# Softmax sums by products with ones, and both heads per instruction, in the first twelve attention units

## The chip, the cores and the metric

One core of a Trainium2 chip runs the whole kernel in one launch. The metric is the device time of the launch in microseconds; lower is better. Engines are TensorE (PE, with its weight loads PEld), VectorE (DVE), ScalarE (ACT), GpSimd (POOL) and SyncE (SP), which here issues the loads and stores.

## The reference

Attention over 8 batches, 8 heads, 576 positions and 64 dimensions, followed by an FFN on the 4608 x 512 result:

```python
scores = scale * np.matmul(q, k.transpose(0, 1, 3, 2))          # scale = 1/8
rel = pos[:, None] - pos[None, :]
mask_plain = (rel >= 0) & (rel < 32)                            # heads 0-3
mask_dil = (rel >= 0) & (rel < 128) & (rel % 4 == 0)            # heads 4-7
scores = np.where(masks, scores, -1e9)
attn = np.exp(scores - scores.max(-1, keepdims=True))
attn = attn / (attn.sum(-1, keepdims=True) + 1e-9)
x = (attn @ v)                                                  # to [4608, 512]
h = np.maximum(np.maximum(x @ w1, x @ w2), x @ w3)              # 512 -> 768
out = h @ w_out                                                 # 768 -> 512
```

q, k, v and the output are float32, the FFN's weights float64.

## The kernel before

**Tiling.** The positions of a batch are cut into two halves of 288 rows, and the heads into four pairs: 16 halves x 4 pairs make 64 attention units, numbered in that order. Pairs 0 and 1 are plain, pairs 2 and 3 dilated. A plain unit has three blocks of 96 queries by 128 keys for each of its two heads, a dilated one four blocks of 72 by 104 (its positions are sorted by remainder mod 4, so that the window is dense). The FFN goes over ten tiles of rows (two of 256, eight of 512), in three products of split numbers: x and the weights are kept as a float32r high part and a rest (xH and xL, wupH and wupL, wdn, h), and high x high, low x high, high x low are summed in PSUM (L815 for the up side, L870 for the down side). x lies in a ring of 1536 rows (xH, xL).

**Two kinds of units.** Units 0 to 11 (LEAN = 12) go through `dense` (L477), units 12 to 63 in pairs through `attention` and `behind` (L648, L681). `dense` puts the mask into PSUM as a product with the identity (L502), adds the scores (L507), and takes the row maxima, one instruction for each head (`most`, L525). Then it does one of two things. Units with u % 4 in (0, 2) (BLOCKWISE) scale the maxima (`eighth`, L531) and take one exponential for each block from PSUM into the buffer W, with the row sums as an accumulator output (`expo_b`, L550). The others subtract the maxima on DVE (`less`, through the helper at L361), take one exponential for each head in SBUF (`expo`, L539), and sum on DVE (`total`, L542). Both then add 1e-9 to the sums (`eps`, L570), take the reciprocals of 6 or 8 columns (`recip`, L573), multiply W by them (`norm`, POOL or DVE, L361), transpose each block on PE (L588), copy the result to PT (`turned`, L354 on ACT or L358 on DVE), and multiply with v (L602). `rounded_of` (L612) writes the output to xH and the rest to xL. Line 354 is the ACT copy helper, L358 the DVE one, L361 the two-tensor helper, whichever engine runs it.

**Weights.** `weight` (L384) is run for 18 up and 6 down weights. They come as float64 (L437), and each is put together on chip: ACT rebiases the high word (L419, into a PSUM bank cp), POOL or DVE extracts three bits of the low word (L424), DVE joins them (L428), one engine writes the high part (L354), and POOL or DVE the rest (L361). All of this lies in the first 85 us.

**What sets the order.** `Plan` (L98) holds every step with a cost for each engine that can do it (`act`, `dve`, `dve2`, `pool1`, `pool`, L364 to L378), its dependences, its buffers and a due time worked backwards from the FFN's products (`deadlines`, with UNIT_PACE, UNIT_SLACK, UNIT_LEAD for attention and WEIGHT_... for weights). `order` (L159) places the steps one by one on the engine's modelled clock, the earliest first and at equal times the one due first, and moves a step to an engine that isn't its usual one if that wins over SPILL = 3.16 us. The kernel issues in that order, and each engine's queue runs in order. PSUM has 6 banks under the tag "b" (scores, transposes, outputs, weights' cp) and 2 for the FFN. Until the first FFN product is placed, idle products (`filler`, L948) are put into PE's gaps, and 16 in a row where the modelled time passes 21 and 35 us (BURSTS).

Of the kernel before, what the change touches and what calls it, by code (L numbers as in the profile page):

```python
# [11 lines left out]
U8 = mybir.dt.uint8  # L12
# [21 lines left out]
LEAN = 12  # L34

BLOCKWISE = (0, 2)


STAGE, STAGE_H = ["wd", "h"], 4
# [26 lines left out]
class Buf:  # L66


    def __init__(self, pool, tag, limit, shape, dtype, name):
        self.pool, self.tag, self.limit = pool, tag, limit  # L70
        self.shape, self.dtype, self.name = shape, dtype, name
        self.users = 0
        self.number = None
        self.end = 0.0
        self.slot = None
        self.t = None

    def take(self):
        if self.t is None and isinstance(self.pool, list):
# [18 lines left out]
class Plan:  # L98
# [48 lines left out]
    def room(self, st, slots):  # L147
# [6 lines left out]
        for tag in set(new):  # L154
            k = new.count(tag)
            at = max(at, sorted(slots[tag])[k - 1][0] if len(slots[tag]) >= k else 1e9)
        return at

    def order(self, fill=None):  # L159
        self.deadlines()  # L160
        self.given = {}
        free = {"pe": 0.6, "act": 4.0, "dve": 4.3, "pool": 3.6, "sp": 0.6}
# [10 lines left out]
        while len(order) - fills < len(self.steps):  # L173
# [43 lines left out]
            for b in st.bufs:  # L217
                if b.slot is None:
                    free_slot = min(slots[b.tag])
                    b.slot = free_slot[1]  # L220
                    slots[b.tag].remove(free_slot)
# [22 lines left out]
            for b in st.bufs:  # L244
                b.users -= 1
                b.end = max(b.end, end)
                if not b.users:
                    slots[b.tag].append((b.end + 0.2, b.slot))
# [21 lines left out]
def tile_dilated_window_attention__then__maxout_ffn(  # L270
# [33 lines left out]
    small_c = const.tile([128, 2], F32, name="small_c")  # L304
    zero, eps_c = small_c[:, :1], small_c[:, 1:]
    nc.gpsimd.memset(eps_c, 1e-9)
    make_identity(nc, ident)
# [7 lines left out]
        "tmp": (4, [128, 512], F32),  # L315
# [10 lines left out]
    BANKS = {"b": 6, "ffn": 2}  # L326

    def buf(tag, name, shape=None, dtype=None):
        if tag in BANKS:
            return Buf(ps, tag, BANKS[tag], [128, 512], F32, name)  # L330
        if tag in KEPT:
            return Buf(KEPT[tag], tag, len(KEPT[tag]), None, None, name)
# [16 lines left out]
    for t in KEPT["W"]:  # L349
        nc.gpsimd.memset(t[:, 768:], 0.0)  # L350
# [33 lines left out]
    def weight(j, before):  # L384

        up = j < NWU
        n = 512
        f = j // 3 if up else j - NWU
        st = buf(STAGE[j % len(STAGE)] if j < STAGE_H else "wd", f"st{j}", [128, 2 * n], F32)
        res = [] if up else [wdn[f]]  # L390

        def part(z):
            return (wupL if z else wupH)[:, j] if up else wdn[f].t[:, z]

        cb, cp = buf("tmp", f"c{j}"), buf("b", f"cp{j}")

        def high():
            return st.t.rearrange("p (n t) -> p n t", t=2)[:, :, 1]

        def cf():  # L400
            return cb.t[:, :n]

        def cw():
            return cb.t.bitcast(U32)[:, :n]

        def pf():
            return cp.t[:, :n]

        def pw():
            return cp.t.bitcast(U32)[:, :n]

        def like(ap):
            return ap.rearrange("p (c m) -> p c m", c=4) if up else ap

        def rebias(_):

            nc.scalar.activation(pf(), high(), AF.Prelu, scale=REBIAS, alpha=SIGN_SHIFT)  # L419

        def low3(e):

            b = st.t.bitcast(U8).rearrange("p (n t) -> p n t", t=8)[:, :, 3]
            (nc.gpsimd if e == "pool" else nc.vector).tensor_scalar(cw(), b, 1 / 32, -31 / 64, ALU.mult, ALU.add)  # L424

        def joined(_):

            nc.vector.scalar_tensor_tensor(  # L428
                cw(), pw(), 3, cw(), op0=ALU.logical_shift_left, op1=ALU.bitwise_or
            )  # L430

        def split(e):
            copy(e, part(0), like(cf()))

        s = plan.add(
# [573 lines left out]
```

## Time and profile before

| | |
|---|---|
| time, median of 3 (lowest to highest) | 725.41 us (725.38 to 725.49) |
| the profiled execution's own time | 725.29 us |
| its span, first to last instruction | 723.4 us |
| PE, PEld busy | 710.1, 585.8 us |
| DVE, ACT, POOL busy | 364.7, 298.1, 231.7 us |
| granted PE clock | 1.00 throughout |
| moved by DMA | 57.46 MB |

Busy time is the union of an engine's instructions. PE's instructions overlap, and their ends are modelled, so the distance from one group's start to the next says more of its cost than a single duration. A row "who <- whom" in a list of waits gives total microseconds, number of times and the longest. A row of a group gives busy microseconds and mean nanoseconds, then idle time of the engine before it and what ended that.

### The profile page before, as it was taken

The page shows a single profiled execution, that of the slowest core. Times are in us where ns is not written, and L with a number is a line of the kernel's source. Part 1 is how long each engine was busy: PE and PEld are TensorE (multiplying, and loading weights), DVE is VectorE, ACT ScalarE, POOL GpSimd, SP SyncE. Part 2 cuts the span into 40 slices and gives each one's busy share as a digit, 9 for nine tenths or more (in the row PEclk, how much of TensorE's full clock was granted, in tenths as well). Part 3 has the DMA queues.
Part 4 walks back from the last instruction along what each step waited for, and adds up shares of the span by engine and source line. Part 5 has one row for each costly group of instructions (what it writes and reads, how often), then busy time and mean ns, then how long its engine had stood idle before and what let it go on. Part 6 is the DMA issues. An engine that isn't in the chain of part 4 may idle for free.

```text
span 723.4 us, 13138 instructions
## 1 busy us (share of the span) xinstructions
PE 710.1 (98%) x4750; PEld 585.8 (81%) x4750; DVE 364.7 (50%) x1419; ACT 298.1 (41%) x1104; POOL 231.7 (32%) x324
## 2 busy tenths in 40 slices
PE   8998999999999999999999999999999999999997
PEld 4677899888888888888888888888888888888886
DVE  5898665565545653666455546655565501101110
ACT  5887854444444334434444444443444311111111
POOL 4998923233223332333223232322223301200110
PEclk9999999999999999999999999999999999999999
DMA  9986232322141203121321223222300010000001
GB/s 321 342 270 201 61 91 59 93 57 65 48 131 45 77 14 108 59 62 61 101 79 58 64 87 94 58 64 72 109 23 24 13 46 1 0 30 30 0 1 58
DMA packets 30368, 57.46 MB, mean 79 GB/s; under 512 B 2912, under 2 KB 11104, under 8 KB 30304
## 3 DMA queue, kind: packets, MB, share of 16 engines
q1 hardware_dynamic: 30304, 56.63, 24.6%
q8 instruction: 37, 0.61, 0.4%
q14 instruction: 27, 0.22, 0.1%
HBM read 47.19 MB, written 9.44 MB: 78 GB/s over the span
## 4 chain that ended last, share of the span: by engine, by line
PE 89%; POOL 4%; DVE 3%; issue 2%; ACT 1%; DMA 1%; SPq 0%; POOLq 0%; DVEq 0%; ACTq 0%
PE u L815 58%; PE d L870 20%; PE s L668 5%; PE pv L774 4%; POOL c L424 1%; POOL wupL L361 1%; DMA k<-in_qk_d_dram 1%; POOL W L361 1%; DVE mx L525 1%; POOL wdn L361 1%; ACT W L550 0%; PE idle L948 0%; DVE c L428 0%; POOL h L361 0%; DVE sm L570 0%
## 5 line engine op out<-in xcount | busy, mean ns | idle before, releaser
L815 PE MATMUL u<-xH,wupH 128*128 128x512 f32 (+1 forms) x720 | 179.6, 371 | 0.4 <-DVE tmp L361 0.2
L815 PE MATMUL u<-xL,wupH 128*128 128x512 f32 (+1 forms) x720 | 178.7, 370 | 0.0
L815 PE MATMUL u<-xH,wupL 128*128 128x512 f32 (+1 forms) x720 | 177.9, 369 | 0.0
L361 DVE TENSOR_TENSOR tmp<-u,tmp 128x512 f32<-128x512 f32 (+1 forms) x120 | 76.4, 637 | 194.4 <-PE u L815 172.1
L870 PE MATMUL d<-wdn,h 128*128 128x512 f32 x648 | 151.9, 392 | 0.1
L691 ACT ACTIVATE W<-W,mx 96x128 f32<-96x128 f32 (+3 forms) x364 | 134.4, 371 | 30.9 <-DVE mx L700 30.6
L815 PEld LDWEIGHTS u<-xH,wupH 128*128 128x128 f32 x720 | 127.0, 188 | 24.5 <-ACT tmp L354 0.4
L815 PEld LDWEIGHTS u<-xL,wupH 128*128 128x128 f32 x720 | 127.4, 188 | 23.7
L815 PEld LDWEIGHTS u<-xH,wupL 128*128 128x128 f32 x720 | 127.7, 188 | 23.0
L870 PEld LDWEIGHTS d<-wdn,h 128*128 128x128 f32 x648 | 120.7, 188 | 26.4 <-POOL wdn L361 0.5
L361 POOL TENSOR_TENSOR h<-tmp,h 128x512 fp32r<-128x512 f32 (+1 forms) x60 | 71.4, 1190 | 215.4 <-ACT h L354 215.4
L762 DVE STREAM_TRANSPOSE PT<-W 32x192 f32<-32x192 f32 (+1 forms) x312 | 125.1, 401 | 16.2 <-POOL W L361 12.2
L354 ACT CAST h<-tmp 128x512 fp32r<-128x512 f32 (+1 forms) x60 | 34.6, 577 | 205.3 <-DVE tmp L361 205.3
L361 POOL TENSOR_TENSOR W<-W,sm 96x384 f32<-96x384 f32 (+3 forms) x126 | 100.3, 815 | 56.9 <-DVE sm L741 50.7
L700 DVE CUSTOM_DVE_ANT_0 W<-s,masks 96x128 f32<-96x128 f32 (+3 forms) x364 | 70.9, 257 | 70.3 <-PE s L668 70.3
L736 POOL TENSOR_TENSOR sm<-sm,small_c 96x6 f32<-96x6 f32 (+1 forms) x52 | 10.4, 200 | 192.0 <-ACT W L691 192.0
L691 ACT ACTIVATION_READ_ACCUMULATOR W<-W,mx 72x1 f32 (+1 forms) x364 | 68.6, 188 | 0.0
L354 ACT COPY tmp<-u 128x512 f32<-128x512 f32 (+1 forms) x60 | 32.6, 544 | 57.7 <-PE u L815 49.7
L354 ACT COPY o<-d 128x512 f32<-128x512 f32 x36 | 21.1, 587 | 84.1 <-PE d L870 84.1
L668 PE MATMUL s<-k 64*96 64x128 f32 (+3 forms) x728 | 38.7, 254 | 0.0
L668 PEld LDWEIGHTS s<-k 64*72 64x72 f32 (+1 forms) x728 | 33.7, 149 | 2.8 <-issue 0.4
L774 PEld LDWEIGHTS pv<-PT,v 104*64 104x64 f32 (+1 forms) x728 | 27.2, 137 | 8.7 <-issue 8.5
(53 smaller groups left out, 387.5 us busy)
## 6 DMA issues: line engine op xcount, KB each, us to landing
k<-in_qk_d_dram SPq DMA_DIRECT2D x32, 352.0 KB, 4.1
k<-in_qk_p_dram SPq DMA_DIRECT2D x32, 304.0 KB, 3.2
st<-in_w_up_dram SPq DMA_DIRECT2D x18, 512.0 KB, 7.2
out_dram<-o SPq DMA_DIRECT2D x36, 256.0 KB, 2.0
v<-in_v_d_dram SPq DMA_DIRECT2D x32, 208.0 KB
v<-in_v_p_dram SPq DMA_DIRECT2D x32, 192.0 KB, 4.2
st<-in_w_dn_dram SPq DMA_DIRECT2D x6, 512.0 KB, 3.8
```

The lines of the kernel that those rows point to most:

```text
L354: nc.scalar.copy(dst, src)
L361: (nc.vector if eng == "dve" else nc.gpsimd).tensor_tensor(dst, a, b, op=op)
L424: (nc.gpsimd if e == "pool" else nc.vector).tensor_scalar(cw(), b, 1 / 32, -31 / 64, ALU.mult, ALU.add)
L525: nc.vector.tensor_reduce(mx.t[:96, m0:m1], S3(j), axis=mybir.AxisListType.X, op=ALU.max, negate=blockwise)
L668: nc.tensor.matmul(banks[j].t[:nq, wk * i : wk * i + nk], kb.t[d, q0 : q0 + nq], kb.t[d, k0 : k0 + nk], start=True, stop=True,)
L691: nc.scalar.activation(a, a, AF.Exp, bias=mx.t[:nq, n : n + 1], scale=-1.0, accum_out=sm.t[:nq, n : n + 1])
L700: nc.vector.tensor_tensor_reduce(W3()[:nq, n, mo : mo + nk], banks[j].t[:nq, wk * i : wk * i + nk], mask[:nq, mo : mo + nk], -0.125, 3e38, ...
L736: nc.gpsimd.tensor_tensor(a, a, eps_c[:nq].broadcast_to([nq, 2 * nb]), op=ALU.add)
L762: nc.vector.transpose(PT.t[c : c + 32, : 2 * nb, 32 * i : 32 * i + 32], W3(e)[32 * i : 32 * i + 32, :, c - e : c - e + 32],)
L774: nc.tensor.matmul(pv.t[64 * j : 64 * j + 64, q0 : q0 + nq], v.t[:wk, j, i, :], PT.t[:wk, nb * j + i, :nq], start=True, stop=True,)
L815: nc.tensor.matmul(bank.t[:, :n], wt[:, 3 * f + g, c, :], (xL if xz else xH)[:, c, r0 : r0 + n], start=(m == 0 and c == 0), stop=(m == 2 a ...
L870: nc.tensor.matmul(bank.t, hs[f].t[:, hz, s0 : s0 + 128], wdn[f].t[:, wz], start=(f == 0 and m == 0), stop=(f == NF - 1 and m == 2),)
```

## The change

In `dense`, for units 0 to 11:

- Scores, transposes and outputs each take a couple of adjacent PSUM banks (one for each head), so `most`, `less`, the exponential and the copy to PT work on both heads in one instruction. The subtraction is an addition of the negated maximum.
- A string FORMS gives the form of each unit: nine "c" (subtraction on DVE, one exponential over both heads) and three "C" (units 2, 10 and 11: scaled maxima and one exponential for each block, without accumulator output). A form "B", which transposes scores instead, is written but used by no unit.
- W is not normalised. After the products with v, the same number of products with a column of ones, broadcast to 64, puts the row sums into the second bank, in the layout of the output. Then `over` adds 1e-9 (ACT or DVE), takes the reciprocal of 128 x 288, multiplies the output by it, and writes xH (ACT, DVE or POOL) and xL (DVE or POOL) from SBUF.
- The 1e-9, the product and the split use the buffers "tmp", which weights and the FFN use too.

Around it: buffers "tmp", "b" and "ffn" become fixed tiles whose slot the planner chooses (`couple`, `single`); six of the weights alternate between the staging buffers wd and h instead of four; a few planner constants differ; W is cleared whole at the start, two buffers on POOL and two on DVE. `weight` is rewritten to take two weights at a time from number COUPLED = 24 on; there are 24 in all, so each is still taken alone.

```diff
-BLOCKWISE = (0, 2)
-STAGE, STAGE_H = ["wd", "h"], 4
+COUPLED = 24
+FORMS = "ccCcccccccCC"
+STAGE, STAGE_H = ["wd", "h"], 6
-UNIT_PACE, UNIT_SLACK, UNIT_LEAD = 1.378, 13.402, 3.655
+UNIT_PACE, UNIT_SLACK, UNIT_LEAD = 1.177, 11.984, 3.655
-WEIGHT_PACE, WEIGHT_SLACK, WEIGHT_LEAD = 0.428, 0.922, 0.773
+WEIGHT_PACE, WEIGHT_SLACK, WEIGHT_LEAD = 0.428, 0.961, 0.972
...
-        free = {"pe": 0.6, "act": 4.0, "dve": 4.3, "pool": 3.6, "sp": 0.6}
+        free = {"pe": 0.6, "act": 4.0, "dve": 5.3, "pool": 5.0, "sp": 0.6}
...
+    ones_c = small_c[:, 2:].broadcast_to([128, 64])
+    couples = [ps.tile([128, 2, 512], F32, name=f"banks_{i}", bufs=1) for i in range(3)]
+    KEPT["b"] = [x[:, i] for x in couples for i in range(2)] + couples
+    KEPT["ffn"] = [ps.tile([128, 512], F32, name=f"bank_{i}", bufs=1) for i in range(2)]
+    tmps = [const.tile([128, 2, 512], F32, name=f"tmps_{i}") for i in range(2)]
...
-    for t in KEPT["W"]:
-        nc.gpsimd.memset(t[:, 768:], 0.0)
+    for i, t in enumerate(KEPT["W"]):
+        (nc.vector if i % 2 else nc.gpsimd).memset(t, 0.0)
...
+        mx = buf("mx", f"mx{u}")
+        sp, tp, pp = (buf("b", f"{x}{u}", width=2) for x in ("s", "pt", "pv"))
+        PT, tmp = buf(f"PT{dil}", f"PT{u}"), buf("tmp", f"sm{u}")
...
+        def most(_):
+            src = sp.t[:nq, :, :nw].rearrange("p j (n k) -> p j n k", k=wk)
+            dst = mx.t[:nq, : 2 * nb].rearrange("p (j n) -> p j n", j=2)
+            nc.vector.tensor_reduce(dst, src, axis=mybir.AxisListType.X, op=ALU.max, negate=True)
...
+        s = plan.add({"dve": dve(2 * nw)}, most, [s], [sp, mx])
...
+            if form == "C":
+                s = plan.add({"dve": 0.165, "pool": 0.22}, eighth, [s], [mx])
...
+                    made.append(plan.add({"act": act(wk)}, expo_b, [s], [sp, W, mx]))
             else:
+                s = plan.add({"dve": dve(2 * nw)}, less, [s], [sp, W, mx])
+                made = [plan.add({"act": act(2 * nw, False)}, exps, [s], [W])]
+            s = plan.add({"pe": 0.1 + 2 * nb * (nq / 1200 + 0.005)}, transposes, made, [W, tp], rows=nq)
+            s = plan.add({"act": act(2 * HALF), "dve": dve(2 * HALF)}, moved, [s], [tp, PT])
 
         def values():
...
+            for i in range(nb):
+                for j in range(2):
+                    nc.tensor.matmul(
+                        pp.t[64 * j : 64 * j + 64, 1, nq * i : nq * i + nq],
+                        ones_c[:wk],
+                        PT.t[:wk, nb * j + i, :nq],
+                        start=True,
+                        stop=True,
+                    )
...
+            s = plan.add({"act": act(HALF), "dve": dve(HALF)}, eps, [s], [pp, tmp])
+            s = plan.add({"dve": dve(HALF)}, lambda _: nc.vector.reciprocal(tmp.t[:, :HALF], tmp.t[:, :HALF]), [s], [tmp])
+            s = plan.add({"dve": dve(HALF)}, lambda _: tt("dve", x(), in_order(0), x(), ALU.mult), [s], [pp, tmp])
...
+            h = plan.add(
+                {"act": act(HALF, False), "dve": dve2(HALF), "pool": pool1(HALF)},
+                lambda e: copy(e, xH[:, p, r0 : r0 + HALF], tmp.t[:, :HALF]),
...
+            l = plan.add(
+                {"dve": dve(HALF), "pool": pool(HALF)},
+                lambda e: tt(
...
-        return values, nb * nq / 600 + 0.08, [vload, *copied], [v, PT, pv], rounded_of(half, p, dil, pv)
+        return values, 2 * nb * nq / 600 - 0.07, [vload, s], [v, PT, pp], over
```

More of the change, by code (lines that the diff above doesn't have):

```diff
@@ L247, in order @@
                 if not b.users:
-                    slots[b.tag].append((b.end + 0.2, b.slot))
+                    slots[b.tag] += [(b.end + 0.2, b.slot + i) for i in range(b.width)]
             for n in st.next:
@@ L451, in weight, with part, src @@
-        return s, l, first
+        s = plan.add({"dve": dve(n * k)}, joined, [*seconds, *firsts], [cp, cb])
+        def part(z, i, m):
+            if up:
+                w = (wupL if z else wupH)[:, js[i] : js[i] + m]
+                return w.rearrange("p j c m -> p (j c m)")
+            return wdn[js[i] - NWU].t[:, z]
+        made = []
+        for i, m in [(0, k)] if up else [(i, 1) for i in range(k)]:
+            def src(i=i, m=m):
+                return both(cb.t) if m == k else one(cb, i)
+            h = plan.add(
+                {"act": act(n * m, False), "dve": dve2(n * m), "pool": pool1(n * m)},
+                lambda e, i=i, m=m, src=src: copy(e, part(0, i, m), src()),
+                [s],
+                [cb, *res],
+            )
+            l = plan.add(
+                {"pool": pool(n * m), "dve": dve(n * m)},
+                lambda e, i=i, m=m, src=src: tt(
+                    e, part(1, i, m), src(), part(0, i, m).bitcast(F32), ALU.subtract
+                ),
+                [h],
+                [cb, *res],
+            )
+            made += [(h, l, firsts[-1])] * m
@@ L454, in loads @@
+        return made
     def loads(u, after):
@@ L513, in scores, with turned @@
+        def turned(_):
+            ones = identb[:nq, :nq].unsqueeze(1)
+            for j in range(2):
+                for z, m in ((nb, 1), (1, 0)) if not (hf or dil) else ((nb, hf),):
+                    nc.tensor.matmul(
+                        T(j)[:, :z],
+                        masks[:nq, m, :wk],
+                        ones.broadcast_to([nq, z, nq]),
+                        start=z == nb,
+                        stop=False,
                         skip_group_check=True,
                     )
+            for i in range(nb):
+                for j, q, k in halves(i):
+                    nc.tensor.matmul(T(j)[:, i], k, q, start=False, stop=False, skip_group_check=True)
@@ L901, in tile_dilated_window_attention__then__maxout_ffn @@
     plan.kind = "w"
-    for j in range(NW):
-        plan.lead = WEIGHT_LEAD
-        w_of[j] = weight(j, w_of[j - 1][2] if j else None)
+    j, plan.lead = 0, WEIGHT_LEAD
+    while j < NW:
+        js = [j] if j < COUPLED else [j, j + 1]
+        for x, made in zip(js, weight(js, w_of[j - 1][2] if j else None)):
+            w_of[x] = made
+        j += len(js)
     prev = None
@@ L945, in tile_dilated_window_attention__then__maxout_ffn @@
     idle = buf("ffn", "idle")
+    idle.slot = 0
     def filler(_):
```

286 lines of the change are left out of this document (152 added, 134 removed).

## The prediction

> **What bounds the kernel now.** I read the page first, then the busy time of the engines by stretch, the order in time of TensorE, its waits, and last the groups of instructions by shape. The page gives the span; the stretches below are cut where TensorE does the first product of FFN tile 0 (31.9), of tile 1 (90.3) and of tile 2 (131).
>
> ```profile
> span 723.4 us, 13138 instructions
> ```
>
> ```profile
> 5.90:31.90 26.00, 24.35 (x249) 14.78 (x247) 21.03 (x50) 21.51 (x71) 17.38 (x21) 1.00 1.02 367
> 31.90:90.30 58.40, 53.51 (x494) 46.25 (x492) 49.04 (x118) 46.42 (x145) 53.29 (x60) 1.00 0.57 187
> 90.30:131.00 40.70, 40.70 (x384) 38.30 (x381) 24.57 (x107) 18.01 (x75) 13.34 (x23) 1.00 0.25 73
> 131.00:723.00 592.00, 588.65 (x3625) 485.28 (x3623) 269.30 (x1143) 212.16 (x815) 145.49 (x207) 1.00 0.18 56
> ```
>
> The columns are length, then busy time of PE, weight load, DVE, ACT, POOL, then granted clock, DMA share and GB/s. From 90.3 on PE is busy without a break (40.70 of 40.70; the 3.35 missing from the last stretch is its tail), at clock 1.00. Nothing that happens on another engine there can shorten the span; a microsecond of PE work added there lengthens it by one. The change touches twelve units that run before that. So the question is what the first 90 us hold. Two things show: the three elementwise engines are all loaded (in 31.9 to 90.3 POOL 53.29 of 58.40, DVE 49.04, ACT 46.42), and PE is hardly idle there either. The waits of PE in that stretch, the four largest, and the largest of DVE:
>
> ```profile
> PE pt L588 <- DVE sm L573: 1.8, 1, 1.8
> PE pt L588 <- ACT W L550: 1.0, 1, 1.0
> PE pv L602 <- issue: 0.6, 1, 0.6
> PE s L502 <- DVE c L428: 0.5, 1, 0.5
> ```
>
> ```profile
> DVE c L428 <- POOL c L424: 5.6, 6, 1.4
> ```
>
> Together 3.9 us of PE waits. The rest of what PE loses lies ahead of tile 0, as idle products that fill its time:
>
> ```profile
> 10.15 1.25 PE L948 MATMUL idle<-masks,identb 128*128 128x512 bf16 x5
> ...
> 12.56 3.19 PE L948 MATMUL idle<-masks,identb 128*128 128x512 bf16 x14
> ...
> 22.61 3.63 PE L948 MATMUL idle<-masks,identb 128*128 128x512 bf16 x16
> ...
> 31.88 0.74 PE L815 MATMUL u<-xH,wupH 128*128 128x256 f32 x4
> ...
> 47.06 0.41 PE L588 MATMUL pt<-ident,W 72*104 72x72 f32 x4
> 47.27 0.72 PE L815 MATMUL u<-xL,wupH 128*128 128x256 f32 x4
> 47.83 0.64 PE L815 MATMUL u<-xH,wupL 128*128 128x256 f32 x4
> ...
> 61.41 0.72 PE L602 MATMUL pv<-PT,v 104*64 104x72 f32 x16
> 62.06 0.74 PE L815 MATMUL u<-xH,wupH 128*128 128x256 f32 x4
> ```
>
> The idle products hold some 8 us (1.25, 3.19, 3.63), and only the wait for the four units of tile 0 lets them in. That makes the first 90 us a race of two nearly equal limits: PE's own work, and POOL with DVE behind it (DVE's largest wait is for POOL's byte extraction of a weight).
>
> **The change, part by part.** The rows for the elementwise work of all twelve units, from the groups by shape up to 95 us:
>
> ```profile
> L361 POOL TENSOR_TENSOR W<-W,sm 96x384 f32<-96x384 f32 x14 | 11.7, 851 | 6.4 <-ACT W L539 3.5 <-DVE sm L573 1.6 <-DVE sm L741 1.1
> L361 POOL TENSOR_TENSOR W<-W,sm 96x416 f32<-96x416 f32 x12 | 10.3, 876 | 1.0 <-ACT PT L354 0.6 <-DVE sm L573 0.3
> L550 ACT ACTIVATION_READ_ACCUMULATOR W<-s,mx 96x1 f32 x42 | 8.2, 196 | 0.0
> L550 ACT ACTIVATE W<-s,mx 96x104 f32<-96x104 f32 x24 | 8.0, 338 | 1.2 <-DVE mx L531 1.2
> L550 ACT ACTIVATE W<-s,mx 96x128 f32<-96x128 f32 x18 | 6.3, 360 | 0.0
> L525 DVE TENSOR_REDUCE mx<-s 96x4 f32<-96x416 f32 x12 | 6.5, 567 | 0.0
> L525 DVE TENSOR_REDUCE mx<-s 96x3 f32<-96x384 f32 x12 | 6.0, 538 | 4.8 <-PE s L507 4.7
> L361 DVE TENSOR_TENSOR xL<-pv,xH 128x288 fp32r<-128x288 f32 x12 | 5.2, 444 | 0.3 <-ACT xH L354 0.3
> L531 DVE TENSOR_SCALAR mx<-mx 96x4 f32<-96x4 f32 x6 | 4.9, 830 | 0.0
> L354 ACT CAST xH<-pv 128x288 fp32r<-128x288 f32 x11 | 4.3, 394 | 0.9 <-PE pv L602 0.9
> L354 ACT COPY PT<-pt 128x288 f32<-128x288 f32 x11 | 4.3, 399 | 0.5 <-PE pt L588 0.4
> L570 DVE TENSOR_SCALAR sm<-sm 96x6 f32<-96x6 f32 x6 | 3.6, 595 | 1.0 <-ACT W L550 1.0
> L570 DVE TENSOR_SCALAR sm<-sm 96x8 f32<-96x8 f32 x6 | 3.5, 579 | 0.4 <-ACT W L550 0.4
> L542 DVE TENSOR_REDUCE sm<-W 96x4 f32<-96x416 f32 x6 | 3.4, 572 | 0.6 <-ACT W L539 0.6
> L361 DVE TENSOR_TENSOR W<-s,mx 96x416 f32<-96x416 f32 x6 | 3.3, 575 | 0.0
> L361 DVE TENSOR_TENSOR W<-W,sm 96x384 f32<-96x384 f32 x2 | 3.2, 1614 | 0.0
> L361 DVE TENSOR_TENSOR W<-s,mx 96x384 f32<-96x384 f32 x6 | 3.1, 536 | 0.0
> L542 DVE TENSOR_REDUCE sm<-W 96x3 f32<-96x384 f32 x6 | 3.0, 528 | 0.0
> L539 ACT ACTIVATE W<-W 96x384 f32<-96x384 f32 x6 | 2.8, 520 | 0.0
> L573 DVE RECIPROCAL sm<-sm 96x8 f32<-96x8 f32 x6 | 1.2, 195 | 0.1
> L573 DVE RECIPROCAL sm<-sm 96x6 f32<-96x6 f32 x6 | 1.1, 176 | 0.0
> ```
>
> *POOL.* The normalising products go: the two POOL rows hold 26 products, 22.0 us. The twelve units have 24, of which two ran on DVE, so four of the 26 belong to later units: 22.0 - 4 x 0.85 = 18.6 us leave. If the last step (xL) falls to POOL now and then, some comes back. POOL stops being a limit.
>
> *ACT.* Out go 42 accumulator reads (8.2), the six blockwise units' exponentials (8.0 and 6.3), twelve whole-head exponentials (2 x about 3.0), 24 PT copies and 12 xH copies (24 x 0.399 + 12 x 0.394 = 14.3): 42.8. In come: nine exponentials over both heads (about 0.9 each by twice 520 less one fixed part: 8.1), 24 blockwise ones at 0.338 (8.1), twelve copies of 576 columns (about 0.65: 7.8), twelve copies of the sums at 0.394 (4.7), twelve xH (4.7): 33.4. ACT gains some 9 us.
>
> *DVE.* Out: maxima 12.5, the eighths 4.9, subtractions 6.4, sums 6.4, the 1e-9 steps 7.1, reciprocals 2.3, two normalisings 3.2, xL 5.2: 48.0. In: twelve maxima over both heads (twice 538 or 567 less a fixed part, about 0.92: 11.0), nine subtractions (about 0.95: 8.6), three eighths (0.6, estimated), twelve products of output and reciprocal at xL's 0.444 (5.3), twelve xL whose two inputs now both lie in SBUF, and twelve reciprocals of 128x288. Two of these are open.
>
> xL with two SBUF inputs: the like of it on DVE is the normalising product at 1614 ns, where 384 columns from PSUM took 536; 288 columns from PSUM took 444. Bounds 0.44 and 1.6; I take 0.8, since POOL will be less busy than when the 1614 was made: 9.6.
>
> The reciprocal is the disputed cost. The plan prices it like any DVE instruction, 0.15 + 0.00105 x 288 = 0.45. The trace shows only 6 and 8 elements: 176 and 195 ns, a slope of 9.5 ns per element, where the subtraction's 536 and 575 ns differ by 1.2 ns per element. With 9.5 throughout 288 columns would cost 2.86; at one column per nanosecond, 0.45. A third reading takes the fixed part of the other DVE rows, about 0.15, from the two times and leaves 4 to 6 ns per element; I take 5.2, or 1.65 us: nearer to the low end of the slope, because six columns measure a slope badly. Twelve make 19.8 (bounds 5.4 and 34.3).
>
> [...]
>
> DVE's sum is then 11.0 + 8.6 + 0.6 + 5.3 + 9.6 + 19.8 = 54.9 against 48.0: 0.6 us more for each unit (bounds -1.0 with both low; +2.6 with both high).
>
> *PE.* One unit's products with v hold PE from 61.41 to 62.06, 0.65. The products with ones have the same count and shape: 0.6 to 0.65 more for each unit, 7.5 in all. Transposing both heads in one go saves one change of work: after a group of transposes the next four FFN products show 0.72 rather than 0.64, so 0.1 for each unit. Net 0.53 a unit. For the four units before 31.9 the idle products, 8 us, cover it; if that cover went, it would cost 2.1. For the eight others it lies in the stretch where PE hardly waits: 8 x 0.53 = 4.2 us.
>
> *What queues behind.* The plan's queues are in order. Each reciprocal runs 1.2 us longer than planned, and behind it on DVE stand the maxima of tile 0's FFN groups, the joins of weights and the next unit's maximum. PE then waits for an FFN bank of which there are two. Against that, the waits on POOL (5.6 for DVE) go. DVE's 49.04 becomes 49.04 + 8 x 0.6 = 53.8 in a stretch of 58.4 + 4.2: 86% where it was 84%. I therefore leave PE's waits at their 3.9, with bounds of 0 and about 8.
>
> *PSUM.* Scores, transposes and outputs now each hold an aligned couple of six banks, the outputs until division is over, and weights break couples by single banks. The row that shows such a wait is the 0.5 of scores for DVE; if every one of the eight units met it, 4 us; if none, zero. I take zero, as DVE's late release is in the waits already.
>
> *Loads.* One more weight may be fetched early: 512 KB at 367 GB/s is 1.4 us that a unit's load may come later in the stretch with DMA at 1.02; zero to 1.4, I take zero, since the SP order still follows due times. The larger memsets of W run while the first load is awaited. The altered pace and slack reorder later units too, under a PE that never waits after 90.3: zero.
>
> **The sum.** Profiled execution: 725.29, of which 723.4 is span and 1.9 lies around it; the median is 725.41, a difference of 0.1 that I ignore. 725.3 + 4.2 (PE) + 0 (waits unchanged) = 729.5; I say 730 for the small bounds that all point upward. Its own range is 727 to 733.
>
> **Rivals.**
> 1. *Faster.* Tile 0 starts sooner and PE's waits vanish. For: ACT (21.51 of 26.00 before 31.9) loses about 3 us over the first four units and POOL's chain link is gone; with a reciprocal near 0.45 DVE is relieved as well. Then tile 0 starts about 3.4 earlier, and 3.9 of waits go: 725.3 + 4.2 - 3.9 - 3.4 = 722.2. Against: the slope of the reciprocal rows, and DVE's 21.03 of 26.00.
> 2. *No change.* The waits go but the start doesn't move: 725.3 + 4.2 - 3.9 = 725.6.
> 3. *Much slower, DVE the limit.* At 2.86 for the reciprocal (and xL as taken), a unit costs DVE 1.8 more: 49.04 + 8 x 1.8 = 63.4, at 93% busy a stretch of 68.2, 9.8 longer; before 31.9, 21.03 + 4 x 1.8 = 28.2, at 93% 30.4, or 4.4 longer than 26.0, half of it in present slack: 725.3 + 9.8 + 2.2 = 737.3. It decides once 49.04 + 8d passes 93% of 62.6, d = 1.15, that is a reciprocal over 2.2 us.
>
> **Chances.** Forecast 0.48, rival one 0.24, two 0.12, three 0.16. A measurement can tell 0.2% (1.45 us) from no change. Faster by more than that: rival one, 0.24. Within: rival two and a sliver of the forecast, 0.13. Slower: 0.63. The range 721 to 738 takes in rival one's middle and rival three's, and leaves out their ends.
>
> **What would show it.** In the profile after: a RECIPROCAL group of 128x288, twelve times, near 1.65 us (0.45 speaks for rival one, over 2.2 for three); twice the products at the line of the outputs; POOL clearly under 53 us between tile 0's and tile 1's first products, DVE above 49; tile 0's first product near 32 and tile 1's near 94; PE without a break after. If tile 1 starts before 89, or PE's waits in that stretch exceed 8 us, the working is wrong at that step.

## The result, and the profile after

| | before | after |
|---|---|---|
| time, median (lowest to highest) | 725.39 us (724.99 to 725.49) | 734.58 us (733.77 to 735.79) |
| the profiled execution's own time, its span | 725.29, 723.4 us | 735.79, 734.0 us |

After is slower: the ratio is 1.0129, 95% interval 1.0112 to 1.0147. That is 9.2 us between the medians, where the forecast was 4.6. The direction was right and the size was not.

The busy times of the engines by stretch, cut at the first products of tiles 0, 1 and 2, have the columns of those of before: length, busy time of PE, weight load, DVE, ACT and POOL, granted clock, DMA share and GB/s.

```profile
7.20:41.80 34.60, 29.87 (x349) 19.57 (x347) 27.77 (x34) 22.25 (x44) 15.19 (x17) 1.00 0.90 312
41.80:101.80 60.00, 55.88 (x586) 49.92 (x585) 48.44 (x95) 42.12 (x107) 39.78 (x44) 0.97 0.50 158
101.80:141.60 39.80, 39.80 (x366) 37.58 (x365) 25.22 (x108) 18.03 (x74) 12.20 (x22) 1.00 0.24 69
141.60:734.00 592.40, 588.62 (x3625) 485.30 (x3623) 269.07 (x1143) 211.51 (x815) 145.36 (x207) 1.00 0.18 55
```

The last row is that of before, to within 0.7 us in every engine: nothing was lost in the steady part. Tile 0 starts at 41.77, not 31.88 (+9.9); the way from tile 0 to tile 1 takes 60.07, not 58.45 (+1.6); that from tile 1 to tile 2 is about 1 shorter. Together +10.6, the difference of the two spans (the profiled run of after is the slowest of its four). Against before, then, nearly all of the lateness is there when tile 0 starts, and DVE works 27.77 of the 34.60 us ahead of it. The reciprocal's own share lies elsewhere in part, as the first experiment shows.

The groups by shape, up to 105 us, show what the new instructions cost (busy us, mean ns, then idle time before them):

```profile
L686 DVE RECIPROCAL tmps<-tmps 128x288 f32<-128x288 f32 x12 | 23.3, 1944 | 3.8 <-ACT tmps L681 3.8
...
L570 DVE TENSOR_REDUCE mx<-banks 96x6 f32<-96x768 f32 x6 | 5.6, 939 | 3.3 <-PE banks L548 3.3
...
L388 DVE TENSOR_TENSOR tmps<-banks,tmps 128x288 f32<-128x288 f32 x12 | 5.4, 451 | 0.5
...
L388 DVE TENSOR_TENSOR xL<-tmps,xH 128x288 fp32r<-128x288 f32 x11 | 5.0, 456 | 1.0 <-ACT xH L381 1.0
```

A reciprocal takes 1944 ns, more than four times a product of the same shape in the row below (451), and more than four times the 0.45 us that the plan counts for it.

PE's waits up to tile 0, and then from tile 0 to tile 1 (who, for whom: us, times, longest):

```profile
PE bank L1052 <- DVE masks L374: 4.3, 1, 4.3
PE banks L545 <- DVE tmps L388: 2.5, 2, 1.2
PE banks L608 <- DVE W L388: 1.3, 1, 1.3
PE banks L608 <- DVE tmps L388: 0.8, 1, 0.8
```

```profile
PE banks L545 <- DVE tmps L388: 1.5, 1, 1.5
PE banks L545 <- DVE tmps L453: 1.4, 1, 1.4
PE banks L608 <- DVE tmps L388: 1.1, 1, 1.1
```

The first line is the start of the program. In the others, `W L388` left aside, PE is held by `tmps L388` or `tmps L453`, a product that ends a division or the join of a weight. They stand on DVE behind a reciprocal and free a bank that PE needs for scores (L545) or transposes (L608). The last reciprocal ahead of tile 0 can be followed in DVE's order in time (start, us, what; idle before in brackets):

```profile
37.85 1.95 DVE L686 RECIPROCAL tmps<-tmps 128x288 f32<-128x288 f32 x1
39.91 0.46 DVE L388 TENSOR_TENSOR tmps<-banks,tmps 128x288 f32<-128x288 f32 x1
40.86 0.46 DVE L388 TENSOR_TENSOR xL<-tmps,xH 128x288 fp32r<-128x288 f32 x1 [0.50 <-ACT xH L381]
```

and on PE:

```profile
22.23 0.72 PE L652 MATMUL banks<-PT,v 104*64 104x72 f32 x16
...
25.94 3.84 PE L1052 MATMUL bank<-masks,identb 128*128 128x512 bf16 x17
...
35.99 0.72 PE L652 MATMUL banks<-PT,v 104*64 104x72 f32 x16
...
40.42 0.55 PE L545 MATMUL banks<-masks,identb 96*96 96x416 bf16 x2 [1.25 <-DVE tmps L388]
40.90 0.94 PE L548 MATMUL banks<-k 64*72 64x104 f32 x16
41.77 0.74 PE L915 MATMUL bank<-xH,wupH 128*128 128x256 f32 x4
```

The outputs of unit 3 (35.99) come 13.8 us after those of the unit before (22.23). Scores of units 4 to 6, transposes of unit 4 and 24 idle products (17 of them in the row shown) lie between. Their reciprocal and product on DVE hold PE once more: it waits 1.25 us for the bank that the product frees at 40.37, then does the scores of unit 7 (40.42 and 40.90), and tile 0 follows at 41.77 without a gap.

### The profile page after: what moved, and what is told of

It is laid out like the page before. It is cut to its first block, busy times and chain, and to the rows that moved or that the text cites. A ratio compares the mean times of both kernels' runs of the same rounds, so it can differ in the third digit from the quotient of the medians.

```text
span 734.0 us, 13339 instructions
## 1 busy us (share of the span) xinstructions
PE 717.1 (98%) x4926; PEld 593.5 (81%) x4926; DVE 374.1 (51%) x1382; ACT 295.2 (40%) x1041; POOL 215.6 (29%) x302
## 4 chain that ended last, share of the span: by engine, by line
PE 90%; DVE 4%; ACT 2%; issue 2%; DMA 1%; POOL 0%; SPq 0%; DVEq 0%; ACTq 0%; POOLq 0%
PE bank L915 59%; PE bank L970 20%; PE banks L768 5%; PE banks L874 4%; DVE tmps L686 1%; DMA v<-in_v_p_dram 1%; DVE tmps L453 1%; ACT banks L431 1%; DVE mx L570 1%; DVE W L388 0%; DVE tmps L388 0%; PE bank L1052 0%; PE banks L548 0%; PE banks L608 0%; PE banks L652 0%
## 5 line engine op out<-in xcount | busy, mean ns | idle before, releaser
L915 PE MATMUL bank<-xH,wupH 128*128 128x512 f32 (+1 forms) x720 | 179.4, 371 | 0.0
L915 PE MATMUL bank<-xH,wupL 128*128 128x512 f32 (+1 forms) x720 | 178.9, 371 | 0.0
L915 PE MATMUL bank<-xL,wupH 128*128 128x512 f32 (+1 forms) x720 | 178.8, 370 | 0.0
L388 DVE TENSOR_TENSOR tmps<-bank,tmps 128x512 f32<-128x512 f32 (+1 forms) x120 | 76.3, 636 | 195.1 <-PE bank L915 172.8
L970 PE MATMUL bank<-wdn,h 128*128 128x512 f32 x648 | 151.5, 391 | 0.0
L915 PEld LDWEIGHTS bank<-xH,wupL 128*128 128x128 f32 x720 | 128.4, 190 | 23.3
L915 PEld LDWEIGHTS bank<-xL,wupH 128*128 128x128 f32 x720 | 127.9, 189 | 23.4
L915 PEld LDWEIGHTS bank<-xH,wupH 128*128 128x128 f32 x720 | 127.7, 189 | 23.3
L970 PEld LDWEIGHTS bank<-wdn,h 128*128 128x128 f32 x648 | 120.8, 188 | 26.1
L388 POOL TENSOR_TENSOR h<-tmps,h 128x512 fp32r<-128x512 f32 (+1 forms) x60 | 70.7, 1178 | 219.8 <-ACT h L381 219.7
L388 POOL TENSOR_TENSOR W<-W,sm 96x384 f32<-96x384 f32 (+2 forms) x104 | 81.5, 802 | 52.6 <-DVE sm L841 52.6
```

The source lines that it names most:

```text
L388: (nc.vector if eng == "dve" else nc.gpsimd).tensor_tensor(dst, a, b, op=op)
L915: nc.tensor.matmul(bank.t[:, :n], wt[:, 3 * f + g, c, :], (xL if xz else xH)[:, c, r0 : r0 + n], start=(m == 0 and c == 0), stop=(m == 2 a ...
L970: nc.tensor.matmul(bank.t, hs[f].t[:, hz, s0 : s0 + 128], wdn[f].t[:, wz], start=(f == 0 and m == 0), stop=(f == NF - 1 and m == 2),)
```

## The experiments

The theories, by the letters that the expectations use. A: the reciprocal, 1.94 us on DVE where 0.45 is planned, is the loss. B: it is the order on PE, scores ahead of unit 3's outputs, that the couples of banks and the plan bring about. C: it is the added products on PE. D: it is the coupling of the banks as such. E: the planner's constants fit the one form of softmax and not the other. Times below are medians; a ratio is against the kernel before, run on the same chip.

**The reciprocal replaced (e1_cheap_div).** A product of the same shape stands in its place, from PSUM, at the same price in the plan and in the same order. The division is left out.

```diff
-            s = plan.add({"dve": dve(HALF)}, lambda _: nc.vector.reciprocal(tmp.t[:, :HALF], tmp.t[:, :HALF]), [s], [tmp])
+            s = plan.add({"dve": dve(HALF)}, lambda _: tt("dve", x(), in_order(1), x(), ALU.mult), [s], [pp, tmp])
```

> The reciprocal of 128x288 is replaced by a product of the sums in PSUM with the same buffer, an instruction of the price that the plan assumes (0.45 us, as the division's product shows); the order of all instructions stays as it is. The division is thus left out and the output is wrong. Theory A (the reciprocal's 1.94 us instead of 0.45, four of them on DVE ahead of tile 0's first product and eight after it, is what costs the time): tile 0 starts at about 41.8 - 4 x 1.5 = 35.8, and the time falls by 6 to 9 us, to 726 to 729. Theory B (the couples of banks: the outputs of unit 3 stand in TensorE's order behind the scores of units 4 to 6 and the idle products, whatever the reciprocal takes): tile 0 starts no earlier than 39, and the time falls by under 3 us, to 732 or more.

Measured 725.70 us, ratio 0.9999 (0.9990 to 1.0008). The whole loss is gone, a little more than A gave, though tile 0 starts at 37.52 where A gave 35.8. The stretches up to tile 1:

```profile
7.20:37.50 30.30, 30.02 (x348) 19.89 (x346) 21.91 (x34) 21.92 (x44) 15.30 (x17) 1.00 0.99 348
37.50:91.70 54.20, 54.03 (x587) 48.26 (x586) 39.64 (x98) 42.38 (x108) 40.17 (x44) 1.00 0.55 177
```

PE has the same instructions as after (348 and 587 where it had 349 and 586), but is idle for 0.28 and 0.17 us where it was idle for 4.73 and 4.12. With these two rows the loss can be added up: 4.45 of idle time ahead of tile 0, 3.95 behind, and 1.85 more busy time behind (55.88 against 54.03), most of it a lowered clock (0.97 in that stretch of after, 1.00 here; last section). That makes 10.25; tile 1 starts 10.16 earlier than in after (91.68 against 101.84). A holds. B, as the cause of the total, falls: unit 3's outputs are late here too, at 33.05.

**The plan told the real price (e2_true_cost).**

```diff
-            s = plan.add({"dve": dve(HALF)}, lambda _: nc.vector.reciprocal(...), [s], [tmp])
+            s = plan.add({"dve": 1.95}, lambda _: nc.vector.reciprocal(...), [s], [tmp])
```

> Only the plan's price of the reciprocal is changed, from 0.45 to 1.95 us; the instructions are the same in another order. Theory A with the accent on the wrong price (queues in an order that waits for DVE): the plan puts other work ahead, and 2 to 4 us come back, 731 to 732.5. Theory A with the accent on the work itself (DVE has 18 us more to do): no gain, 734 to 736. Theory B (couples are held while the division is under way): the plan now sees them held longer, starts tile 0 later still, 735 to 738.

Measured 732.95 us, ratio 1.0101 (1.0086 to 1.0116); tile 0 starts at 44.51, tile 1 at 98.74. About 1.6 us come back of 9.2, between the two forecasts of theory A. In this plan the wrong price is the small part of the loss, the work itself the large one.

**The order forced (e6_cheap_order).** e1 again (division left out), and the scores of units 4 and later are planned only after unit 3's outputs.

```diff
-            {"pe": 0.3 + ...}, scores, [kload], [kb, mx, sp], rows=96
+            {"pe": 0.3 + ...}, scores, [kload, first.get(3) if u > 3 else None], [kb, mx, sp], rows=96
...
-                    x_of[divmod(u, NPAIR)] = products([dense(u)])[1][0](waits(u // NPAIR))
+                    first[u], xs = products([dense(u)])
+                    x_of[divmod(u, NPAIR)] = xs[0](waits(u // NPAIR))
```

> The run with the cheap instruction in the place of the reciprocal (725.7, output not divided) once more, with one thing added to the plan: the scores of units 4 and up may be placed only after the output products of unit 3, so that these no longer stand behind three units' scores on TensorE. Theory B's remainder (with the reciprocal gone, tile 0 still starts 5.6 us later than before, at 37.5, and that is the order): tile 0 starts at 28 to 33, and the time falls by 2 to 5 us, to 721 to 724. If the units 4 to 7 then come later by as much, it is given back: 725 to 727.

Measured 733.99 us, ratio 1.0115 (1.0100 to 1.0130): 8.3 us worse than e1, where at worst 727 was expected. PE in order of time:

```profile
22.86 9.24 PE L1053 MATMUL bank<-masks,identb 128*128 128x512 bf16 x41
32.03 0.72 PE L652 MATMUL banks<-PT,v 104*64 104x72 f32 x16
...
43.38 0.72 PE L915 MATMUL bank<-xH,wupH 128*128 128x256 f32 x4
```

Unit 3's outputs come at 32.03 though no scores stand ahead of them: 41 idle products do. So the early scores of units 4 to 6 do not hold unit 3 back; they fill a gap that is there anyway, and tile 0 and what follows lose by leaving them out. What puts unit 3's outputs there is the plan's reckoning of a load. The times that `Plan` works out are the same in after and in e6: the copy to PT of unit 3 ends at 18.6, but its v, issued behind nine weights, counts as landed only at 29.1, and the products are placed right behind that (at 29.9 and at 29.1). No run moved this load, so what an earlier one would bring isn't known.

**The two halves of the change (f1_ones_only, f4_ones_cheap, f2_both_heads_only).** f1 is the kernel before with the sums by ones and the division at the end alone: `total`, `norm` and the small reciprocals go, a second bank pw takes the sums, and `over` stands as in the change.

```diff
-        pv = buf("b", f"pv{u}")
+        pv, pw = buf("b", f"pv{u}"), buf("b", f"pw{u}")
...
+                        pw.t[64 * j : 64 * j + 64, nq * i : nq * i + nq],
+                        ones_c[:wk],
...
-        return values, nb * nq / 600 + 0.08, [vload, *copied], [v, PT, pv], rounded_of(half, p, dil, pv)
+        return values, 2 * nb * nq / 600 - 0.07, [vload, *copied], [v, PT, pv, pw], over
```

> The kernel before with one half of the change alone: products with ones give the sums into a bank of their own, the output is divided at the end by the same three instructions, and no sums, small reciprocals or normalising of W are left; each head keeps its own instructions and the planner's constants and buffers are those of before. Theory A (the reciprocal of 128x288): all of the loss is in this half, 732 to 737. Theory D (the loss comes from coupling the banks, which makes steps wait for adjacent pairs): this half alone is near the time of before, 724 to 728.

Measured 737.42 us, ratio 1.0167 (1.0152 to 1.0182): 12.0 us slower, more than the whole change. Its twelve reciprocals take 1943 ns each, and PE's largest wait ahead of tile 1 is again for DVE, 3.8 us for the product behind a reciprocal.

f4 is f1 with the reciprocal replaced as in e1 (the division left out); one bank is held for a step longer.

```diff
-            s = plan.add({"dve": dve(HALF)}, lambda _: nc.vector.reciprocal(...), [s], [tmp])
+            s = plan.add({"dve": dve(HALF)}, lambda _: tt("dve", x(), in_order(1), x(), ALU.mult), [s], [pw, tmp])
```

> The kernel before with products with ones and a division at the end, each head with its own instructions (737.4), and the reciprocal replaced by a product of the price that the plan assumes; output wrong. Theory A (only the reciprocal): the 12 us come back, 724 to 727, tile 0 at 31 to 35. Theory D (coupled banks delay tile 0 by 5.6 us even without the reciprocal): here, without couples, tile 0 starts at 31 to 33; with them it was 37.5. If tile 0 starts at 36 or later here too, the delay comes from the longer chain behind the output products, not from the couples.

Measured 724.86 us, ratio 0.9992 (0.9983 to 1.0001): 12.6 us faster than f1. A is shown a second time, without any coupling. The stretches up to tile 1:

```profile
5.90:32.90 27.00, 25.09 (x309) 17.26 (x312) 20.55 (x46) 23.48 (x64) 14.18 (x15) 1.00 1.03 377
32.90:93.40 60.50, 58.55 (x662) 51.89 (x659) 46.92 (x120) 47.55 (x129) 41.11 (x46) 1.00 0.55 178
```

Tile 0 starts at 32.86, where e1, with all the rest of the change, has 37.52; e1 then needs 54.2 to tile 1 where f4 needs 60.5. The two stretches don't hold the same work (587 instructions of PE against 662), so only the totals compare: they are level, and nothing of e1's later start is left at the end.

f2 is the other half: after, with W normalised as before and no ones.

```diff
+                made = [plan.add({"dve": dve(2 * nw)}, total, [s], [W, sm])]
+            s = plan.add({"dve": 0.165, "pool": 0.22}, eps, made, [sm])
+            s = plan.add({"dve": 0.18}, recip, [s], [sm])
+            made = [plan.add({"pool": 0.13 + 0.00188 * 2 * nw, "dve": dve(2 * nw)}, norm, [s], [W, sm])]
...
-        return values, 2 * nb * nq / 600 - 0.07, [vload, s], [v, PT, pp], over
+        return values, nb * nq / 600 + 0.08, [vload, s], [v, PT, pv], rounded_of(half, p, dil, pv)
```

> The changed kernel with the other half alone: both heads in one instruction over couples of banks, new constants, memsets and staging as in the changed kernel, but W normalised before it is transposed, with sums on ACT or DVE, reciprocals of 6 or 8 columns and one product for both heads; the output is taken from one bank as before. Theory A: no 128x288 reciprocal, so near the time of before, 722 to 728. Theory D (coupled banks): 730 or more.

Measured 730.70 us, ratio 1.0070 (1.0054 to 1.0087): 5.3 us slower. The halves cost 12.0 and 5.3, the whole 9.2: they don't add up. In f2 tile 0 starts at 37.86, as late as in e1, and tile 1 at 95.3, 5 us later than in before. So a delay of some 6 us ahead of tile 0 belongs to this half of the change, with either softmax; e1 makes it good by tile 1, f2 doesn't. D is not refuted for the normalised form; what in this half makes the delay stays open, but for the next run.

**The constants (e4_old_constants, f3_heads_old_constants).** Staging, paces, slacks and the planner's start times of before, put into after (e4) and into f2 (f3, which also clears all of W on DVE).

```diff
-STAGE, STAGE_H = ["wd", "h"], 6
+STAGE, STAGE_H = ["wd", "h"], 4
...
-UNIT_PACE, UNIT_SLACK, UNIT_LEAD = 1.177, 11.984, 3.655
+UNIT_PACE, UNIT_SLACK, UNIT_LEAD = 1.378, 13.402, 3.655
...
-        free = {"pe": 0.6, "act": 4.0, "dve": 5.3, "pool": 5.0, "sp": 0.6}
+        free = {"pe": 0.6, "act": 4.0, "dve": 4.3, "pool": 3.6, "sp": 0.6}
```

> The changed kernel with the planner constants and the staging of before (pace, slack, lead, 4 staged weights, first free times). Theory A: the constants only shuffle an order that DVE limits, within 2 us of 734.6. Theory B (the order of scores and outputs on TensorE, set by these constants together with the couples): the order of the first units changes and the time moves by more than 3 us, either way.

> The run with both heads in one instruction and no products with ones (730.7) with the planner constants and staging of before and all W buffers cleared on DVE. Theory D (coupled banks): 728.5 to 731, as only the memsets' 0.9 comes back. Theory E (the loss of that half is its constants, which fit the other softmax): 724 to 727.

Measured 735.13 us, ratio 1.0133 (1.0118 to 1.0148), the same as after; and 736.64 us, ratio 1.0156 (1.0139 to 1.0174), 5.9 worse than f2 and outside both forecasts, in part at a lower clock (mean 0.991 against 0.997). E explains nothing of the loss of after. For f2 the constants of the change were the better ones, so they aren't what costs its 5.3 us either. Another order of the same work thus moved the time by 6 us here, and by 8 in e6.

**Products with ones left out (e5_no_ones).** The sums are not computed; the output itself goes into the reciprocal.

```diff
-                    nc.tensor.matmul(
-                        pp.t[64 * j : 64 * j + 64, 1, nq * i : nq * i + nq],
-                        ones_c[:wk],
...
-                    nc.scalar.activation(x(), in_order(1), AF.Identity, bias=eps_c)
+                    nc.scalar.activation(x(), in_order(0), AF.Identity, bias=eps_c)
```

> The products with ones are left out, and the output is divided by itself instead of by the sums, so the output is wrong; all other instructions stay. The plan's price of the product step is left as it is, so the order stays. TensorE has 12 x 0.6 = 7.2 us less to do. Theory C (TensorE's added work sets the time, as the prediction's sum had it for eight units): 734.6 - 4.8 = 729.8 or less. Theory A (DVE is the limit ahead of tile 1): the four units ahead of tile 0 bring up to 0.6 in the chain of the last one, the eight others under 2 us, as the stretch from tile 0 to tile 1 grew only by 1.6: 732 to 734.

Measured 734.52 us, ratio 1.0115 (1.0098 to 1.0132): no gain from some 7 us of PE work less. C as the cause would have shown one. It isn't a clean proof, since the clock was lower in this run (mean 0.990 against 0.998):

```profile
40.00:44.00 4.00, 2.71 (x19) 1.84 (x19) 3.27 (x5) 2.61 (x6) 1.30 (x2) 0.61 0.58 154
44.00:48.00 4.00, 4.00 (x21) 4.00 (x21) 3.40 (x5) 2.52 (x6) 2.58 (x3) 0.53 0.95 334
```

**The memsets of W (e3_memset_dve).** All four on DVE.

```diff
-        (nc.vector if i % 2 else nc.gpsimd).memset(t, 0.0)
+        nc.vector.memset(t, 0.0)
```

> All four buffers W are cleared on DVE after the masks, none on POOL. In the changed kernel the cast of the masks took 1745 ns beside two POOL memsets of 807 ns, in the one before 465 ns, and the first scores began 1.3 us later. Theory A and theory B alike, if that delay is carried to the end: first scores at about 5.9, time 733.3. If later waits absorb it: 734.6, no change.

Measured 733.72 us, ratio 1.0110 (1.0095 to 1.0125). DVE's cast of the masks, which took 1.75 us in after, is short again:

```profile
2.32 0.43 DVE L373 CAST masks<-PT 128x512 bf16<-128x512 f32 x1 [0.68 <-POOL PT L370]
```

The first scores are back at 5.89, from 7.21, and tile 0 starts at 41.26. The 0.9 us of gain lie within the overlap of the two intervals.

**The reciprocal doubled (e7_two_recips).** A second one follows the first, at no cost in the plan; the output is no longer divided by the sums.

```diff
+            s = plan.add({"dve": 0.0}, lambda _: nc.vector.reciprocal(tmp.t[:, :HALF], tmp.t[:, :HALF]), [s], [tmp])
```

> The reciprocal is taken twice, the second time at a plan price of zero, so each unit costs DVE another 1.94 us; the output is multiplied by the sums and wrong. Theory A: as one reciprocal cost 9 us above the cheap instruction (1.5 us for each of twelve, 18 us of DVE), the second, 23 us of DVE, costs 10 to 14 more: 744 to 749. If DVE had slack left that hides it: 738 to 742.

Measured 762.03 us, ratio 1.0506 (1.0490 to 1.0521): 27.5 us above after, for 23.4 us of DVE work:

```profile
L687 DVE RECIPROCAL tmps<-tmps 128x288 f32<-128x288 f32 x12 | 23.4, 1947 | 0.2
```

```profile
PE banks L545 <- DVE tmps L388: 8.3, 5, 3.2
PE banks L608 <- DVE tmps L388: 5.8, 2, 2.9
```

The direction is A's, the size is more than A gave. The first set of twelve cost 10.2 us of span for 17.9 us more of DVE work (12 x 1.49). Part of that may have fallen into DVE's idle time, as A has it; no run separates it. The second cost more than its own duration, with PE's waits on DVE longer and a mean clock of 0.979.

**Two other ways to divide (g2_ln_exp, g8_small_recip).** Both clear W on DVE. g2 takes the reciprocal on ACT, as the exponential of the negated logarithm.

```diff
-            s = plan.add({"act": act(HALF), "dve": dve(HALF)}, eps, [s], [pp, tmp])
-            s = plan.add({"dve": dve(HALF)}, lambda _: nc.vector.reciprocal(...), [s], [tmp])
+            s = plan.add({"act": act(HALF)}, log, [s], [pp, tmp])
+            s = plan.add({"act": act(HALF, False)}, power, [s], [tmp])
```

> The changed kernel with another division: ACT takes the logarithm of the sums from PSUM (1e-9 as its bias, in the place of the copy that added it) and the exponential of its negative, so the reciprocal leaves DVE and ACT gets one instruction of about 0.44 us more for each unit; the plan prices it so. All W buffers are cleared on DVE. Theory A (the reciprocal on DVE is the loss, and the rest of the change is worth about as much as it costs): at least as good as the run with the cheap instruction, 722 to 726, unless tables have to be loaded in between (1.28 us each in the profile), then 735 or more. Theory D (coupled banks cost 5 us, which the run with both heads alone suggests): 728 or more.

Measured 753.04 us, ratio 1.0389 (1.0368 to 1.0409). ACT loads tables for the two functions in turn, 24 loads more than the single one of after:

```profile
L680 ACT ACT_TABLE_LOAD x12 | 15.4, 1283 | 0.8 <-PE banks L661 0.6
L683 ACT ACT_TABLE_LOAD x9 | 11.5, 1283 | 0.2
L603 ACT ACT_TABLE_LOAD x3 | 3.8, 1283 | 0.8 <-PEq L1102 0.7
```

Twelve stand at the logarithm's line (L680), one for each of its twelve instructions, and the other twelve at those of an exponential (L683, L603); each took 1283 ns, 30.7 us in all. So g2 tells nothing of a division on ACT without them.

g8 sums by products with one column, takes a reciprocal of 6 or 8 columns, and lets PE spread it to the layout of the output.

```diff
+                nc.tensor.matmul(pp.t[:nq, 1, 300 + n : 301 + n], PT.t[:wk, n, :nq], small_c[:wk, 2:], ...)
...
+                            sm.t[:nq, n : n + 1].broadcast_to([nq, 64]),
+                            ident[:nq, :nq],
```

> The changed kernel with the reciprocal made small: products of PT with one column of ones give the sums of a block as one column of 96 or 72 partitions, DVE adds 1e-9 and takes reciprocals of 6 or 8 columns (0.17 and 0.19 us), and TensorE spreads them over 64 partitions by a product with the identity; ACT copies them out and DVE multiplies. All W buffers are cleared on DVE. Theory A: DVE is rid of 1.6 us a unit, TensorE does about as much as before plus 0.3, the chain has one more turn between DVE and TensorE (about 1 us): 723 to 728. If the time stays at 732 or more, it is not DVE's load but the length of the chain behind the outputs.

Measured 744.95 us, ratio 1.0278 (1.0259 to 1.0298), 17 us above the forecast's upper end. DVE lost its long instruction, and now waits itself, for the sums from PE:

```profile
DVE sm L679 <- PE banks L660: 14.9, 11, 2.7
```

But PE doesn't wait for DVE: behind the program's start its waits come to 0.3 us up to 110, and from 50 to 110 it is busy without a break. Tile 0 starts at 45.23, 7.7 us later than in e1, with idle products ahead of it; there the chain may be what is long, as the expectation said. From tile 0 to tile 1 (112.77) PE needs 67.5 us where e1 needs 54.2, and there the loss is PE's own work: a unit's products with one column hold it for 1.04 us and the spreading for another 0.65, where the ones took about 0.67 in all. The expectation had PE at 0.3 more.

No version beat both kernels; those that come level with before (e1, f4) leave the division out.

## Why the prediction was wrong

**The step that failed** is "for the four units before 31.9 the idle products, 8 us, cover it", and with it "+ 0 (waits unchanged)" and tile 0's start near 32: it came at 41.77, and tile 1's, said near 94, at 101.84. The cover was counted for PE alone. DVE's load ahead of tile 0 was worked out (21.03 + 4 x 1.8 of 26.0), but only for rival three; at the 1.65 us of the forecast, too, each reciprocal adds 1.2 us there to an engine at 81% (21.03 of 26.0) that takes its work in the order of issue: the 1018 records of DVE in after start in the order in which the kernel issues them, none ahead of its turn. The idle products didn't absorb that: they stand on PE, which sat idle for 4.73 us there. The runs put 4.25 us of tile 0's delay on the reciprocal (41.77 against e1's 37.52). The other 5.6 (37.52 against 31.88) belong to the rest of the change, which the prediction had at nothing as well; f4, without coupling, forms, constants and whole memsets, starts at 32.86. Half of the 5.6 is in the plan itself, which places tile 0 at 31.7 in before and at 34.5 in after and e1; the memsets' share is 0.5 (41.77 against 41.26 in e3); the rest stays open. Behind tile 0 the reciprocal cost another 5.8 us in waits (3.95) and busy time (1.85, most of it a clock of 0.97), and e1 shows that without it the rest of the change would have come out level.

**The reciprocal** was put at 1.65, and is 1.94. Its bounds held, and the plan's 0.45 is refuted. The third reading had the right form: (1944 - 195) / 280 is 6.2 ns for each further element, outside its 4 to 6 by a little.

**PE's 4.2 us** were right for a unit, not for the stretch. The ones cost what was said, here in e1 between tile 0 and tile 1, seven units:

```profile
L661 PE MATMUL banks<-PT,small_c 104*64 104x72 f32 x64 | 2.7, 226 | 0.0
...
L661 PE MATMUL banks<-PT,small_c 128*64 128x96 f32 x36 | 2.0, 246 | 0.0
```

4.7 us for seven is 0.67 each. Transposes fell from 6.8 us for eight units in before (3.4 and 3.4) to 4.1 for six:

```profile
L588 PE MATMUL pt<-ident,W 72*104 72x72 f32 x32 | 3.4, 228 | 1.8 <-DVE sm L573 1.8
L588 PE MATMUL pt<-ident,W 96*128 96x96 f32 x24 | 3.4, 253 | 1.3 <-ACT W L550 1.0 <-POOL W L361 0.2 <-DVE c L428 0.2
```

```profile
L608 PE MATMUL banks<-ident,W 72*104 72x72 f32 x32 | 2.8, 230 | 0.0
...
L608 PE MATMUL banks<-ident,W 96*128 96x96 f32 x12 | 1.3, 245 | 0.0
```

That is 0.85 and 0.68 a unit, a saving of 0.17 where 0.1 was forecast; net 0.50 a unit, where 0.53 was. Yet PE's busy time between the tiles grew by 0.5 only (53.51 to 54.03). The stretch holds the outputs of seven units, not eight, in before as in e1, and two units' transposes now lie ahead of the later start of tile 0. That leaves 4.7 - 2.7 = 2.0; the other 1.5 lie in the remaining rows and were not taken apart.

**PE's waits between the tiles** were said to stay at 3.9 (the four largest; bounds 0 and 8) and are 4.0 (1.5 + 1.4 + 1.1). But they are other waits than before. Without the reciprocal they vanish (0.17 in e1), as rivals one and two said, and e1 ends at 725.70 where rival two gave 725.6, though not by its way: the start did move, by 5.6, and the stretch to tile 1 became 4.3 shorter. In after the reciprocal puts waits of the same length in place of those that went. That the total agreed with "unchanged" was chance.

**DVE's sum.** xL from two SBUF inputs took 456 ns, the low bound, not 0.8 us. The two errors, 4.1 us too much for twelve xL and 3.5 too little for twelve reciprocals, nearly cancel; DVE's load was about right. The 1614 ns that stood for the high bound of xL were the mean of two instructions of before, 804 and 2423 ns, both beside a busy POOL (66.7 to 69.9); that a less busy POOL brings such a time down was the author's estimate, and no run shows it apart. "DVE above 49" between the tiles was not met by a little (48.44).

**Small steps.** "POOL clearly under 53" holds (39.78), and POOL isn't a limit any more. PE has no break from tile 1 on, and the steady stage is unchanged: both right. The memsets "while the first load is awaited" were not hidden. DVE's cast of the masks (2.32 to 4.07) ran beside POOL's two memsets (2.23 to 3.78), and the first scores came at 7.21, not 5.91. The cast in before, and in after:

```profile
2.29 0.47 DVE L346 CAST masks<-PT 128x512 bf16<-128x512 f32 x1 [0.68 <-POOL PT L343]
```

```profile
2.32 1.75 DVE L373 CAST masks<-PT 128x512 bf16<-128x512 f32 x1 [0.68 <-POOL PT L370]
```

**Rival three** had the engine right, not the place or the point. It decided on DVE's capacity behind tile 0, above 2.2 us. There DVE is busy for 48.44 of 60.0, 81% where the rival needed 93%, and PE still lost 4 us: the delay comes from where in the queue the long instruction stands, not from a full engine. Ahead of tile 0 it gave 2.2, and the runs 4.25.

## What to carry to other kernels

When an instruction becomes longer on an in-order engine, cost it in each stage by what stands behind it and which bank or buffer that frees, before asking whether the engine is full; filler on the engine that waits was no cover here. A function that costs several times a product for each element belongs where the data are narrow: 8 columns at 195 ns are cheap, the same sums spread over 288 columns are 1944 ns, where a product of that width took 451. But count what it costs to bring them there and back: in g8 it cost more than it saved (744.95 us against 734.58). To tell whether an edit's loss is its work or its order, put a cheap instruction in the place of the dear one and keep the order.

## What the runs showed of the hardware

**The clock fell behind a wait of 1.5 us.** In after PE's granted clock is 0.53 from 62.40 to 66.00, behind the 1.49 us wait that ends at 61.20:

```profile
62.40:66.00 3.60, 3.60 (x21) 3.52 (x18) 1.98 (x3) 2.21 (x4) 3.08 (x4) 0.53 0.84 288
```

```profile
61.20 0.53 PE L545 MATMUL banks<-masks,identb 96*96 96x384 bf16 x2 [1.49 <-DVE tmps L388]
...
62.48 1.12 PE L915 MATMUL bank<-xH,wupL 128*128 128x256 f32 x4
63.40 1.05 PE L915 MATMUL bank<-xH,wupH 128*128 128x256 f32 x4
64.25 1.05 PE L915 MATMUL bank<-xL,wupH 128*128 128x256 f32 x4
65.11 1.05 PE L915 MATMUL bank<-xH,wupL 128*128 128x256 f32 x4
65.96 0.32 PE L915 MATMUL bank<-xH,wupH 128*128 128x256 f32 x1
```

Four groups take 3.48 us (62.48 to 65.96) where such groups elsewhere in after start 0.48 apart (110.48, 110.96, 111.44): 1.6 us lost besides the wait itself. The fall came 1.4 us behind the end of the wait: the granted clock was 1.00 from 60.00 to 62.60, 0.50 from 62.60 to 66.00, and 1.00 again from 66.00 to 70.00. A wait of 1.39 that ended at 51.37 was followed by a clock of 1.00 up to 60, and one of 1.81 in before, which ended at 59.33, by 1.00 to the end. So the length of one wait alone doesn't decide it, and no run here shows what does.

**A cast beside a memset.** The same cast took 0.47 us in before, beside four POOL memsets of 96x88 (237 ns each), 1.75 in after beside two of 96x856, 807 ns each, and 0.43 in e3, where POOL has none of them. e3 differs from after in these memsets alone, so the long ones on the other engine cost the cast 1.3 us; the short ones of before show no such cost.

**One column cost more than 96.** In g8 the six products of a unit with one column each (12 records) hold PE for 1.04 us (16.26 to the next start at 17.30); the six with 96 columns ahead of them took 0.64 (15.62 to 16.26). The stationary side differs too: with one column moving it is PT, 128*96, where the products with v have 128*64. No run separates the two, so where the 0.4 us more come from was not shown.

```profile
15.62 0.72 PE L652 MATMUL banks<-PT,v 128*64 128x96 f32 x12
16.26 1.18 PE L660 MATMUL banks<-small_c,PT 128*96 128x1 f32 x12
17.30 0.81 PE L1065 MATMUL bank<-masks,identb 128*128 128x512 bf16 x3
```
